# First chunk of a linear attention and gated FFN kernel: VectorE's work ordered behind an earlier gate product, a task's loads ahead of weight loads

## The chip, the cores and the metric

The kernel runs on one core of a Trainium2 chip. The core has TensorE (matmuls), VectorE, ScalarE, GpSimd, and SyncE, which issues the DMAs. The metric is the device time in microseconds of one execution; the median of three runs is given.

## The reference

A linear attention is followed by a gated feed-forward layer. The softmax of q runs over the 64 elements of a head, that of k over the 576 positions.

```python
# q, k, v: (8, 8, 576, 64) float32
q_s = softmax(q, axis=-1); k_s = softmax(k, axis=2)
kv = einsum('bhsd,bhse->bhde', k_s, v)
x = einsum('bhsd,bhde->bhse', q_s, kv)      # then rows of 512: (4608, 512)
out = (x @ w_a) * (x @ w_b) @ w_out          # d_ff = 1536
```

The weights arrive as float64 and are turned into float32 on the chip.

## The kernel before

The 4608 rows are worked on in nine chunks of 512. Later chunks use a fast matrix product with seven products per pair of 128-wide tiles of d_ff; the first chunk, which the change touches, does it plainly, tile by tile, while it converts the weights.

The first chunk has twelve tiles f of 128 columns of d_ff. For tile f, "gate f" is 24 matmuls (L510) into two PSUM banks, `k0` for x @ w_a and `k1` for x @ w_b. ScalarE copies the first bank into `ga` (`gate_half`, L517), VectorE multiplies it by the second (`gate_end`, L521, the "product of gate f"), and `project_first` (L545) multiplies the result by w_out. Gate f+1 writes the same two banks, so its first half needs ScalarE's copy of gate f and its second half needs the product of gate f.

A float64 weight block becomes float32 in `float_parts`: two ScalarE casts (L103, L104), a VectorE shift (L107), a GpSimd addition (L110), a VectorE join (L113). For w_a and w_b a split into an upper part (ScalarE, L79, or L920 in the startup) and a lower part (VectorE, L82, or L925) follows, which gate f reads; blocks of w_out are split by `split_wo` only for the later chunks. Buffers are few: four `wr`, eight `wy`, eight `ws`, eleven `xo`, which raw weights share.

Beside this, "tasks" prepare the attention for the next chunk: keys (0, 1, 3 and 5), queries (2, 4, 6 and 7), and one key task of a later batch (8). A task has a load, a softmax part (`soft`: for keys a maximum L292 and an exponential; for queries a maximum L358, eight short exponentials L361, L365, L366 and a GpSimd product L367), a transpose on TensorE (`turn`) and a product.

Up to gate 2 the steps stand in an order written out by hand, and `in_order` keeps that order on ScalarE, VectorE and GpSimd (and for the first loads on SP). `in_order` also fixes TensorE's order through the whole first chunk. Everything else is placed by a scheduler at build time, which simulates the engines and may put an instruction of a later loop pass into any gap of an engine's queue; each engine then works its queue strictly in that order. `tc.issue_after(ins)` holds instructions that are traced in its block, and run on the engine of `ins`, behind `ins` in that order; instructions of other engines are free.

The loop over f from 2 to 11 traces, in each pass, the loads of tile f+2, the conversion of w_out's block f, the conversion of w_a and w_b for tile f+1, a load of task f-1, the turn of task f-3, the softmax part of task f-2, gate f (from f = 3), the product of task f-3, and the projection of tile f-1. The lines around the change are these:

```python
    tasks[0][0]()
    load_f(3)
    tasks[1][0]()
```

They stand in the prologue, so task 1 is loaded there, and in the loop's first pass (n + 2 = 1) once more. Before, the softmax parts were held only behind the last splits of the startup, `startup[0]` on ScalarE and `startup[1]` on VectorE. In the last pass the first two blocks of w_out are split and the operands of chunk 1 are made (`x_operands`, with L484 to L494), while GpSimd adds up weights for the fast product (`sums`, L225).

Of the kernel before, what the change touches and what calls it, by code (L numbers as in the profile page):

```python
# [13 lines left out]
ALU = mybir.AluOpType  # L14
# [15 lines left out]
def linear_attention_then_gated_ffn(  # L30
# [18 lines left out]
    nc = tc.nc  # L49
# [4 lines left out]
    NF = 2 * NI  # L54
# [21 lines left out]
    def split(hi, lo, src, hi_engine="act"):  # L76

        if hi_engine == "act":
            nc.scalar.copy(out=hi, in_=src)  # L79
        else:  # L80
            nc.vector.tensor_copy(out=hi, in_=src)
        return nc.vector.tensor_tensor(out=lo, in0=src, in1=hi.bitcast(F32), op=ALU.subtract)  # L82
# [4 lines left out]
    def float_parts(raw, y=None):  # L87

        top = raw.bitcast(F32).rearrange("p (n t) -> p n t", t=2)[:, :, 1]
        low = raw.bitcast(U32).rearrange("p (n t) -> p n t", t=2)[:, :, 0]
        if y is None:
            y = sb.tile([P, DM], F32, name="wy", bufs=8)
        r = sb.tile([P, DM], I32, name="wr", bufs=4)
        u = raw.bitcast(I32)[:, 0:DM]
        yi = y.bitcast(I32)  # L100

        def both():
            nc.scalar.activation(out=y, in_=top, func=AF.Copy, scale=2.0 ** -112)  # L103
            nc.scalar.activation(out=r, in_=low, func=AF.Copy, scale=2.0 ** -29)  # L104

        def shift():
            nc.vector.tensor_single_scalar(u, yi, 3, op=ALU.logical_shift_left)  # L107

        def add():
            nc.gpsimd.tensor_tensor(out=r, in0=u, in1=r, op=ALU.add)  # L110

        def join():
            nc.vector.scalar_tensor_tensor(  # L113
                out=yi, in0=yi, scalar=-(2 ** 31), in1=r, op0=ALU.bitwise_and, op1=ALU.bitwise_or
            )

        return y, (both, shift, add, join)

    def to_float(raw):
        y, parts = float_parts(raw)  # L120
        for part in parts:
            part()
        return y
# [3 lines left out]
    def load_f(f):  # L127

        i, r = divmod(f, 2)
        for half in range(2):  # L130
            raw = sb.tile([P, DM], I64, name="raw", tag="xo", bufs=11)
            ins = nc.sync.dma_start(out=raw, in_=w_ab[i, r, half])
            raws[f, half] = raw
        raw = const.tile([P, DM], I64, name=f"wo{f}_raw", tag=f"wo{f}")
        with tc.issue_after(ins.ins):
            nc.sync.dma_start(out=raw, in_=w_out[f])
        raws[f, "o"] = raw
        return ins
# [3 lines left out]
    def wo_home(f):  # L142
        if f > 3:
            return None
        if f > 1:
            if "mr" not in raws:
                raws["mr"] = sb.tile([P, 2, DM], F32, name="yo", tag="mr", bufs=2)
            return raws["mr"][:, f - 2]
        return sb.tile([P, DM], F32, name=f"yo{f}", tag=f"u{f + 2}", bufs=1)

    def keep_wo(f, y):
        if f > 3:
            w = const.tile([P, 2, DM], F32R, name=f"wo{f}_w", tag=f"wo{f}")
            nc.sync.dma_start(out=w[:, 1].bitcast(F32), in_=y)
            wo[f] = w
            y = w[:, 1].bitcast(F32)
        wo_first[f] = y

    def convert_wo(f):
        y, parts = float_parts(raws.pop((f, "o")), wo_home(f))  # L160
        for part in parts:
            part()
        keep_wo(f, y)

    def split_wo(f):
        if f < 4:
            wo[f] = const.tile([P, 2, DM], F32R, name=f"wo{f}_w", tag=f"wo{f}")
        split(wo[f][:, 0], wo[f][:, 1], wo_first[f])
# [14 lines left out]
    def convert_ab(f, half):  # L183

        keep_ab(f, half, *whole_ab(f, half, to_float(raws.pop((f, half)))))

    def whole_ab(f, half, y):
        w = ws_tile()
        yv = y.rearrange("p (n c f) -> p n c f", n=2, c=2)
        split(w[:, :, 0], w[:, :, 1], yv)  # L190
        return y, w

    def keep_ab(f, half, y, w):
        i, r = divmod(f, 2)
        dy[i, r, half] = dr.tile([P, DM], F32, name=f"dy{i}{r}{half}")
        nc.sync.dma_start(out=dy[i, r, half], in_=y)
        op = ((A11, A12), (None, A22))[r][half]
        if op is not None:
            put_w(i, op, w)
        blocks[f, half] = w  # L200
# [301 lines left out]
    def gate_banks(tags):  # L502
        return [ps.tile([P, T], F32, name=f"pt{n}", tag=tag) for n, tag in enumerate(tags)]

    def gate_part(f, x, n, pairs, pt):

        for g in pairs:
            w = blocks[f, g // 2][:, n, :, g % 2]
            for i, (wp, xp) in enumerate(((0, 0), (0, 1), (1, 0))):
                nc.tensor.matmul(  # L510
                    pt, w[:, wp], x[g][:, xp],
                    start=(g == 0 and i == 0), stop=(g == NP - 1 and i == 2),
                )
# [4 lines left out]
        return ga  # L518

    def gate_end(ga, pt):  # L520
        nc.vector.tensor_tensor(out=ga, in0=pt, in1=ga, op=ALU.mult)  # L521

    def g_split(f, g):
        gh = sb.tile([P, T], F32R, name=f"gh{f % 2}", bufs=1)
# [207 lines left out]
    def key_task(g):  # L732
        box = {}

        def load():
            box["k"] = k_load_t(1, g)
            box["v"] = v_load(1, g)

        def soft():
            kv_exp_t(box["k"])  # L740

        def turn():
            box["e"], copy = kv_turn(box["k"], ("k2", "at"))
            return [copy]

        def prod():
            kv_whole(1, g, box["e"], box["v"], "at")

        return load, soft, turn, prod

    def query_task(g):
        box = {}

        def load():
            box["q"] = q_load(1, g)

        def soft():
            q_soft_first(box["q"])

        def turn():  # L760
            box["e"], copy = q_whole(box["q"], "k2", g % 2)
            return [copy]

        def prod():
            px = x_whole(1, g, box["e"], "at")
            nc.scalar.copy(out=xfs[1][:, g], in_=px)

        return load, soft, turn, prod

    def late_key_task(g, tag="k2"):  # L770
        box = {}

        def load():
            box["k"] = k_load(2, g)
            box["v"] = v_load(2, g)

        def soft():
            box["m"] = kv_max(box["k"])

        def turn():  # L780
            box["m"] = kv_max_turn(box["m"], tag)

        def back():
            kv_exp(box["k"], kv_max_all(box["m"], tag))

        def prod():
            kv_split(2, g, kv_product(box["k"], box["v"], "at"))

        return load, soft, turn, back, prod

    tasks = [key_task(0), key_task(1), query_task(0), key_task(2), query_task(1), key_task(3),
             query_task(2), query_task(3)] + [late_key_task(g) for g in range(1)]
# [13 lines left out]
    at = {}  # L806

    class Startup:
# [153 lines left out]
            at["ga", f] = gate_half(f, at["pt", f][0])  # L962

        def G(f):
            gate_end(at["ga", f], at["pt", f][1])

    x0 = [None] * NP
    traced = nc.cur_bb.bb.instructions
# [35 lines left out]
    startup = [at["last", 0].ins, at["last", 1].ins]  # L1004

    po = at["po"]
    pending = (1, at["ga", 1])
    for f in range(2, NF):
        if f + 2 < NF:
            load_f(f + 2)  # L1010
        convert_wo(f)
        if f + 1 < NF:
            convert_ab(f + 1, 0)
            convert_ab(f + 1, 1)


        n = f - 3
        if n + 2 < NF - 3:
            tasks[n + 2][0]()
        if n < 0:  # L1020
            copies = ()
        else:
            copies = tasks[n][2]()
        if n + 1 < NF - 3:
            with tc.issue_after(startup[0]), tc.issue_after(startup[1]):
                tasks[n + 1][1]()
        if f == NF - 1:
            split_wo(0)
            split_wo(1)
            sy[0] = sums(0)  # L1030
            x_operands(xfs[1], early + late, xo)
        if f > 2:
            pts = gate_banks(("k0", "k1"))
            for h in range(2):
                gate_part(f, x0, h, range(NP), pts[h])
                if h == 0:
                    with ExitStack() as pinned:
                        for copy in copies or ():
                            pinned.enter_context(tc.issue_after(copy.ins))
                        at["ga", f] = gate_half(f, pts[0])  # L1040
            gate_end(at["ga", f], pts[1])
        if n >= 0:
            tasks[n][3]()
        project_first(*pending, po)
        pending = (f, at["ga", f])
# [16 lines left out]
    for c in range(1, NCH):  # L1062
# [4 lines left out]
        for i in range(NI):  # L1067
# [32 lines left out]
            end = c == NCH - 1 and i == NI - 1  # L1100
# [78 lines left out]
```

## Time and profile before

| | |
|---|---|
| time, median of 3 runs | 979.13 us (978.07 to 979.45) |
| the profiled execution | 979.73 us, span 977.9 us |
| TensorE busy (matmul) | 946.1 us, 97% of the span |
| TensorE busy (weight load) | 846.8 us, 87% |
| VectorE busy | 626.7 us, 64% |
| ScalarE busy | 392.0 us, 40% |
| GpSimd busy | 112.3 us, 11% |
| TensorE's mean granted clock | 0.993 of full |

The span is the profile's stretch from the first to the last instruction; the time holds what lies around it too. Shares are means over the whole span, of which the first chunk is some 17%. In the trace PE is TensorE, DVE VectorE, ACT ScalarE, POOL GpSimd, and SP or SPq SyncE and its queue; L521 is line 521 of the kernel. A row of a timeline shows where an instruction starts, how long it lasts, what it writes and reads, and in brackets how long its engine was idle before it and what ended the wait.

### The profile page before, as it was taken

The numbers are of one execution on the slowest core, as the hardware profiler recorded it, in microseconds if no ns is written. First come the engines' busy times: TensorE is split into PE (matmuls) and PEld (weight loads), VectorE is DVE, ScalarE is ACT, GpSimd is POOL, SyncE is SP. The second block draws the span as 40 slices with busy tenths as digits, with TensorE's granted clock in tenths as the row PEclk, the third lists the DMA queues.
The fourth block names the chain that finished last, engine by engine and source line by source line (L and its number), as shares of the span: only waits on it lengthen the run. The fifth ranks groups of instructions, "written<-read, shape, count | busy, mean of one in ns | idle before, by whom it ended". The sixth has DMA issues, their size and how long they took to land.

```text
span 977.9 us, 16984 instructions
## 1 busy us (share of the span) xinstructions
PE 946.1 (97%) x6159; PEld 846.8 (87%) x6159; DVE 626.7 (64%) x1241; ACT 392.0 (40%) x1085; POOL 112.3 (11%) x96
## 2 busy tenths in 40 slices
PE   5879999899999999999999999999999999999998
PEld 4656666799999999999999999999999999999997
DVE  6985777986686656666576566565666446653433
ACT  7875764552363324432442235223623263221101
POOL 3453344332000000000000000000000000000000
PEclk9989999999999999999999999999999999999999
DMA  9999675989898977997699779877988688767761
GB/s 344 412 380 341 238 242 198 408 306 352 290 334 280 361 253 248 334 359 264 240 343 340 257 256 339 299 304 257 331 276 293 236 314 274 271 219 279 255 206 56
DMA packets 97874, 283.26 MB, mean 290 GB/s; under 512 B 11712, under 2 KB 12288, under 8 KB 97792
## 3 DMA queue, kind: packets, MB, share of 16 engines
q1 hardware_dynamic: 97792, 282.18, 80.4%
q8 instruction: 49, 0.80, 0.3%
q14 instruction: 33, 0.27, 0.1%
HBM read 242.06 MB, written 37.98 MB: 286 GB/s over the span
## 4 chain that ended last, share of the span: by engine, by line
PE 80%; DMA 8%; DVE 5%; issue 3%; POOL 2%; ACT 2%; SPq 1%; POOLq 0%; DVEq 0%
PE po L556 27%; PE ka L535 13%; PE kp L535 13%; PE kx L535 13%; PE ky L535 7%; PE pk L312 3%; PE px L466 2%; DMA dw<-ws 2%; POOL wr L110 2%; DMA qts<-in_q 1%; PE pt L510 1%; DMA wo_raw<-in_w_out 1%; DMA vt<-in_v 1%; DMA mr<-dq 1%; PE po L545 1%
## 5 line engine op out<-in xcount | busy, mean ns | idle before, releaser
L556 PE MATMUL po<-wo_w,gh 128*128 128x512 f32 x768 | 230.1, 396 | 0.0
L535 PE MATMUL kx<-xo,ws 128*128 128x256 f32 x1152 | 162.8, 283 | 1.0 <-DVE cc L1110 0.8
L535 PE MATMUL ka<-xo,ws 128*128 128x256 f32 x1152 | 161.4, 283 | 0.8 <-DVE u L1095 0.8
L556 PEld LDWEIGHTS po<-wo_w,gh 128*128 128x128 f32 x768 | 138.6, 188 | 26.8 <-ACT gh L79 0.6
L535 PE MATMUL kp<-xo,ws 128*128 128x256 f32 x1152 | 157.2, 283 | 1.4 <-DVE u L1095 1.4
L535 PEld LDWEIGHTS ka<-xo,ws 128*128 128x128 f32 x1152 | 149.7, 188 | 4.9 <-DVE u L1095 1.0
L535 PEld LDWEIGHTS kx<-xo,ws 128*128 128x128 f32 x1152 | 149.3, 188 | 4.0 <-DVE cc L1110 1.0
L535 PEld LDWEIGHTS kp<-xo,ws 128*128 128x128 f32 x1152 | 146.9, 188 | 3.8 <-issue 1.6
L556 PE MATMUL po<-wo_w,gl 128*128 128x512 f32 x384 | 139.2, 395 | 0.0
L79 ACT CAST gh<-cc 128x512 fp32r<-128x512 f32 x96 | 57.5, 620 | 131.5 <-DVE cc L1119 118.0
L1118 DVE TENSOR_TENSOR cc<-kp,u 128x512 f32<-128x512 f32 x48 | 33.2, 691 | 102.3 <-PE kp L535 102.3
L1109 ACT COPY cc<-kx 128x256 f32<-128x256 f32 x48 | 17.8, 371 | 180.9 <-PE kx L535 174.3
L380 ACT ACTIVATE qt<-qt,st 128x64 f32<-128x64 f32 x224 | 74.9, 338 | 27.6 <-DVE st L377 21.5
L556 PEld LDWEIGHTS po<-wo_w,gl 128*128 128x128 f32 x384 | 71.5, 188 | 16.5 <-DVE gl L82 0.4
L510 PE MATMUL pt<-xo,ws 128*128 128x512 f32 x288 | 75.4, 418 | 9.8 <-DVE ga L521 5.0
L510 PEld LDWEIGHTS pt<-xo,ws 128*128 128x128 f32 x288 | 56.0, 198 | 25.2 <-DVE ga L521 5.4
L535 PE MATMUL ky<-xo,ws 128*128 128x256 f32 x576 | 77.4, 283 | 0.3 <-DMA ws<-dw 0.3
L1108 DVE TENSOR_TENSOR cc<-kp,u 128x512 f32<-128x512 f32 x48 | 32.9, 686 | 68.1 <-PE kp L535 67.9
L535 PEld LDWEIGHTS ky<-xo,ws 128*128 128x128 f32 x576 | 71.8, 188 | 1.1 <-issue 0.5
L82 DVE TENSOR_TENSOR gl<-cc,gh 128x512 fp32r<-128x512 f32 x96 | 66.9, 704 | 8.3 <-ACT gh L79 8.1
L244 POOL PARTITION_ALL_REDUCE mx<-m x20 | 14.7, 736 | 460.2 <-DVE m L255 421.7
L1094 ACT COPY u<-kx 128x512 f32<-128x512 f32 x48 | 28.0, 583 | 82.0 <-PE kx L535 82.0
(144 smaller groups left out, 1202.7 us busy)
## 6 DMA issues: line engine op xcount, KB each, us to landing
ws<-dw SPq DMA_DIRECT2D x312, 512.0 KB, 5.4
dw<-ws SPq DMA_DIRECT2D x42, 512.0 KB, 6.2
mr<-dq SPq DMA_DIRECT2D x112, 128.0 KB, 3.9
raw<-in_w_ab SPq DMA_DIRECT2D x24, 512.0 KB, 7.5
vt<-in_v SPq DMA_DIRECT2D x29, 325.0 KB, 7.4
out<-ot SPq DMA_DIRECT2D x36, 256.0 KB, 5.0
qt<-in_q SPq DMA_DIRECT2D x32, 256.0 KB, 5.4
kt<-in_k SPq DMA_DIRECT2D x24, 320.0 KB, 5.3
```

Source lines behind the costliest of these rows:

```text
L79: nc.scalar.copy(out=hi, in_=src)
L82: return nc.vector.tensor_tensor(out=lo, in0=src, in1=hi.bitcast(F32), op=ALU.subtract)
L110: nc.gpsimd.tensor_tensor(out=r, in0=u, in1=r, op=ALU.add)
L312: nc.tensor.matmul(pk, kt[:, j].rearrange("p h d -> p (h d)"), vt[:, j], start=(j == 0), stop=(j == J - 1),)
L380: nc.scalar.activation(out=qt[:, j, h], in_=qt[:, j, h], func=AF.Exp, bias=st[:, h, 0, j:j + 1], accum_out=st[:, h, 1, j:j + 1],)
L466: nc.tensor.matmul(px[:, s], w, m[:, s], start=(i == 0), stop=(i == 2))
L510: nc.tensor.matmul(pt, w[:, wp], x[g][:, xp], start=(g == 0 and i == 0), stop=(g == NP - 1 and i == 2),)
L535: ins = nc.tensor.matmul(pt[:, n], w[:, n, wp, c], x[:, xp, c], start=(first and n == 0 and i == 0), stop=(i == 5), skip_group_check=True,)
L556: ins = nc.tensor.matmul(po[t], a[:, ts], wo[f][:, w], start=(f == 0 and i == 0), stop=(f == NF - 1 and i == 2),)
L1094: nc.scalar.copy(out=u2, in_=kx)
L1108: nc.vector.tensor_tensor(out=cc[:, 3], in0=kp, in1=u3, op=ALU.add)
L1118: nc.vector.tensor_tensor(out=cc[:, 1], in0=kp, in1=u2, op=ALU.add)
```

## The change

- The product of each gate is kept in `at["end", f]`, those of the startup and those of the loop.
- In pass f the conversions of w_out's block f and of tile f+1 are traced inside `issue_after(at["end", f - 2].ins)`. That instruction runs on VectorE, so their VectorE steps (shift, join, lower part) stand behind the product of gate f-2.
- The softmax part of task f-2 stands, with its VectorE steps, behind the product of gate f-2 (in pass 2, behind that of gate 1) instead of behind the last split of the startup. Its ScalarE steps stay behind `startup[0]`.
- The splits of w_out's blocks 0 and 1 stand, with their VectorE half, behind the product of gate 10.
- A task's load is traced ahead of `load_f(f + 2)`, under the condition `1 < f - 1 < NF - 3`, so tasks 2 to 8 are loaded in passes 3 to 9, and task 1 only in the prologue.

```diff
@@ -518,7 +518,7 @@
         return ga
 
     def gate_end(ga, pt):
-        nc.vector.tensor_tensor(out=ga, in0=pt, in1=ga, op=ALU.mult)
+        return nc.vector.tensor_tensor(out=ga, in0=pt, in1=ga, op=ALU.mult)
 
     def g_split(f, g):
         gh = sb.tile([P, T], F32R, name=f"gh{f % 2}", bufs=1)
@@ -962,7 +962,7 @@
             at["ga", f] = gate_half(f, at["pt", f][0])
 
         def G(f):
-            gate_end(at["ga", f], at["pt", f][1])
+            at["end", f] = gate_end(at["ga", f], at["pt", f][1])
 
     x0 = [None] * NP
     traced = nc.cur_bb.bb.instructions
@@ -1006,27 +1006,30 @@
     po = at["po"]
     pending = (1, at["ga", 1])
     for f in range(2, NF):
+        if 1 < f - 1 < NF - 3:
+            tasks[f - 1][0]()
         if f + 2 < NF:
             load_f(f + 2)
-        convert_wo(f)
-        if f + 1 < NF:
-            convert_ab(f + 1, 0)
-            convert_ab(f + 1, 1)
+
+        with tc.issue_after(at["end", f - 2].ins):
+            convert_wo(f)
+            if f + 1 < NF:
+                convert_ab(f + 1, 0)
+                convert_ab(f + 1, 1)
 
 
         n = f - 3
-        if n + 2 < NF - 3:
-            tasks[n + 2][0]()
         if n < 0:
             copies = ()
         else:
             copies = tasks[n][2]()
         if n + 1 < NF - 3:
-            with tc.issue_after(startup[0]), tc.issue_after(startup[1]):
+            with tc.issue_after(startup[0]), tc.issue_after(at["end", max(f - 2, 1)].ins):
                 tasks[n + 1][1]()
         if f == NF - 1:
-            split_wo(0)
-            split_wo(1)
+            with tc.issue_after(at["end", f - 1].ins):
+                split_wo(0)
+                split_wo(1)
             sy[0] = sums(0)
             x_operands(xfs[1], early + late, xo)
         if f > 2:
@@ -1038,7 +1041,7 @@
                         for copy in copies or ():
                             pinned.enter_context(tc.issue_after(copy.ins))
                         at["ga", f] = gate_half(f, pts[0])
-            gate_end(at["ga", f], pts[1])
+            at["end", f] = gate_end(at["ga", f], pts[1])
         if n >= 0:
             tasks[n][3]()
         project_first(*pending, po)
```

## Rows read from the trace of the kernel before

**Rows 1.** Page, part 2: the span in 40 equal slices, tenths.
```profile
PE   5879999899999999999999999999999999999998
...
PEclk9989999999999999999999999999999999999999
```

**Rows 2.** TensorE's order of time: start us, us, engine line op, tiles, shapes, count, [idle before].
```profile
43.61 0.74 PE L510 MATMUL pt<-xo,ws 128*128 128x512 f32 x2 [1.74 <-ACT ws L920]
46.18 6.92 PE L510 MATMUL pt<-xo,ws 128*128 128x512 f32 x22 [1.83 <-DVE ws L925]
...
60.27 3.04 PE L510 MATMUL pt<-xo,ws 128*128 128x512 f32 x12
68.30 5.49 PE L510 MATMUL pt<-xo,ws 128*128 128x512 f32 x12 [4.99 <-DVE ga L521]
...
132.42 5.83 PE L510 MATMUL pt<-xo,ws 128*128 128x512 f32 x24
...
143.55 5.82 PE L510 MATMUL pt<-xo,ws 128*128 128x512 f32 x24
...
163.04 0.49 PE L271 MATMUL pmx<-m,ones 128*128 128x128 f32 x2 [1.68 <-DVE m L265]
```

**Rows 3.** Busy time by windows: engines, granted clock, DMA share, GB/s.
```profile
47.00:48.00 1.00, 1.00 (x4) 0.81 (x3) 1.00 (x3) 1.00 (x4) 0.00 (x0) 0.50 1.01 406
...
68.00:70.00 2.00, 1.71 (x4) 1.43 (x5) 1.77 (x4) 1.13 (x3) 0.74 (x1) 0.50 0.96 325
```

**Rows 4.** VectorE's order of time up to gate 2's product.
```profile
34.92 0.68 DVE L82 TENSOR_TENSOR wo_w<-yo,wo_w 128x512 fp32r<-128x512 f32 x1
...
37.66 1.86 DVE L107 TENSOR_SCALAR wo_raw<-yo 128x512 int32<-128x512 int32 x2
...
44.97 1.15 DVE L925 TENSOR_TENSOR ws<-wy,ws 128x512 fp32r<-128x512 f32 x1
...
46.77 1.26 DVE L358 TENSOR_REDUCE qst<-qt 128x8 f32<-128x512 f32 x2
...
50.92 2.39 DVE L82 TENSOR_TENSOR wo_w<-yo,wo_w 128x512 fp32r<-128x512 f32 x2
...
62.50 1.51 DVE L107 TENSOR_SCALAR raw<-wy 128x512 int32<-128x512 int32 x1
...
64.14 1.24 DVE L365 TENSOR_SCALAR qst<-qst 128x8 f32<-128x8 f32 x1
...
67.56 0.68 DVE L521 TENSOR_TENSOR ga<-pt,ga 128x512 f32<-128x512 f32 x1
```

**Rows 5.** ScalarE's order of time ahead of gate 2's copy.
```profile
47.62 0.33 ACT L361 ACTIVATE qt<-qt,qst 128x64 f32<-128x64 f32 x1
...
58.73 0.34 ACT L361 ACTIVATE qt<-qt,qst 128x64 f32<-128x64 f32 x1
...
59.56 0.58 ACT L517 COPY ga<-pt 128x512 f32<-128x512 f32 x1
```

**Rows 6.** SP's queue, order of time.
```profile
38.25 0.33 SPq L285 DMA_DIRECT2D kt<-in_kt  x1
```

**Rows 7.** Waits of SP's queue, 0 to 200 us: total, times, longest.
```profile
SPq L285 <- PE pk L312: 2.9, 1, 2.9
```

**Rows 8.** VectorE's order of time, later tiles and the change of chunks.
```profile
106.61 0.69 DVE L521 TENSOR_TENSOR ga<-pt,ga 128x512 f32<-128x512 f32 x1 [0.92 <-PE pt L510]
...
119.60 1.17 DVE L82 TENSOR_TENSOR ws<-wy,ws 128x512 fp32r<-128x512 f32 x1 [0.66 <-ACT ws L79]
...
141.73 0.65 DVE L521 TENSOR_TENSOR ga<-pt,ga 128x512 f32<-128x512 f32 x1
...
149.48 0.69 DVE L521 TENSOR_TENSOR ga<-pt,ga 128x512 f32<-128x512 f32 x1 [5.24 <-PE pt L510]
...
151.61 1.76 DVE L489 TENSOR_TENSOR xt<-xf 128x512 f32<-128x512 f32 x1
```

**Rows 9.** GpSimd's order of time at the change of chunks.
```profile
146.99 12.64 POOL L225 TENSOR_TENSOR ws_y<-ws_y 128x512 f32<-128x512 f32 x8 [3.91 <-DMA ws_y<-dy]
```

## The prediction

> **What bounds the kernel now.** I read the slices of the page first. Each slice is 24.4 us. TensorE is busy nine tenths or more from the fourth slice on, but for the eighth, and the third slice (48.9 to 73.3 us) stands out: seven tenths busy, and the only one whose granted clock is under nine tenths [rows 1]. The first eight slices hold the first chunk and the change to the second; behind them TensorE runs through. A change in the first chunk is therefore worth what it does to TensorE's idle time and clock there, and the 780 us behind it only move. I then read TensorE's own order of time in the first chunk [rows 2]. Its order is fixed by the code, so each idle stretch names what was late. Three stretches matter. Gate 2 (tile f=2) waits 1.74 us for ScalarE's upper part of a weight (L920) and 1.83 us for VectorE's lower part (L925). The second half of gate 3 waits 4.99 us, from 63.31 to 68.30, for VectorE's product of gate 2 (L521), which frees its PSUM bank. At the change of chunks the product pmx waits 1.68 us for VectorE (L265). Behind the first two the granted clock is 0.50 [rows 3], the lower of the two levels, 1.2 GHz.
>
> Last I read VectorE's order ahead of that late product [rows 4]. Gate 2's matmuls are over by 53.1 us (46.18 + 6.92), yet the product starts at 67.56. VectorE is not waiting for it: it works through an in-order queue in which pieces of much later tiles stand in front.
>
> **The change part by part.**
>
> *A. The product of gate 2.* Loop pass f now puts its VectorE conversions and its task's exponents behind the product of tile f-2 (at least tile 1 for the exponents). Before gate 2's product only passes 2 and 3 may now stand. What leaves its front, with the durations of [rows 4]: the statistics of two query tasks, which belong to passes 4 and 6 (1.26 us for two maxima, then two additions of 1.24 us each, of which the last is shown), the split of w_out block 0 (half of the 2.39 us of two splits, 1.20), and the first shift of tile 5's weights (1.51). Together 1.26 + 2 x 1.24 + 1.20 + 1.51 = 6.45 us; durations overlap by some 0.07 us in a row, so I count 6.1. The product moves from 67.56 to at most 61.5 and ends by 62.2, in front of the 63.31 at which TensorE wants the bank. It also needs ScalarE's copy of the first half, which starts at 59.56 [rows 5]. That copy stood behind 16 short exponentials of the same two query tasks, 0.33 us each, 5.3 us in all; they need the statistics just moved, so they leave too, and the copy can come near 54 us. TensorE's wait of 4.99 us goes. Hiding margin: 63.31 - 62.2 = 1.1 us; if that cover is gone, every us of lateness is one of TensorE.
>
> *B. The clock behind that wait.* Twelve matmuls took 5.49 us behind the wait and 3.04 us in front of it [rows 2]; the clock was 0.50 in the first case [rows 3]. Without the wait: 5.49 - 3.04 = 2.45 us back. The Trainium skill, "TensorE: Matmul & The Clock Gate", section "What's actually happening", says that how many matmuls run cold behind an idle stretch varies from run to run; no run here repeats this stretch. By that rule the term could be left out, and the sum would end 2.45 us higher. I take the row. A + B = 7.44 us.
>
> *C. Gate 2 itself.* Before its last weight part (VectorE at 44.97) stood one w_out split (0.68, block 1, at 34.92) and one of the two w_out shifts at 37.66 (half of 1.86, 0.93), both of the loop and both now behind gate 0's product [rows 4]. The shift also starts a GpSimd addition in the same stretch. So the part comes 1.6 us earlier at least by these two. Bounds: below nothing gained (the scheduler may put other unpinned work there), above both waits and the slow clock, 1.74 + 1.83 + 6.92 - 22/24 x 5.83 = 5.15 us (5.83 is 24 matmuls at full clock [rows 2]). I take 2.5, half of it, above the 1.6 since the clock would follow.
>
> *D. Splits of w_out 0 and 1.* They leave stretches where VectorE was ahead of need and come behind gate 10's product (149.48), just where VectorE makes the operands of the next chunk [rows 8]. A two-input VectorE operation takes 0.68 us there or, while GpSimd's eight additions run (146.99 to 159.63 [rows 9]), 1.76 us [rows 8]. Bounds: 0, if they are put behind the operands; 2 x 1.76 = 3.5, if all of it reaches the wait of pmx (163.04 [rows 2]), which ends on VectorE. I take 2 x 0.68 = 1.4: two operations more in a row push the last two of the row out of GpSimd's stretch, where they are fast. The Trainium skill, "GPSIMD Engine Reference", section "1. Specifications", says that GpSimd shares its SBUF interfaces with VectorE instructions that have two SBUF inputs; by that alone both splits would cost the slow price, 3.5, and the sum would end 2.1 us higher. The rows show both prices on the two sides of the additions' end.
>
> *E. Loads.* A task's load (one DMA for a query, two for a key) now stands in front of pass f's three weight loads on SP's queue instead of behind them. A key load that waits for its buffer holds SP: 2.9 us once [rows 7], and behind it stand weight loads and the write-backs that free conversion buffers. Raw weights are loaded some tiles ahead of their conversion, so I take 0; what would be late next is a conversion, with 12 us of lead (below). One thing falls away: task 1 was loaded in the prologue and again in pass 2 (kt at 38.25 [rows 6], then vt), 320 and 325 KB by their shapes. At 406 GB/s [rows 3] that is 1.6 us of full queues. TensorE waits for VectorE and ScalarE there, not for loads, so I take 0; bounds 0 and 1.6 gained.
>
> *F. The conversions held back.* From tile 6 on they already stood behind the product of the tile two before. Tile 9: product 6 at 106.61, its last weight part at 119.60 to 120.77, gate 9 at 132.42 [rows 2, 8]. So a chain takes 13.5 us behind the product (120.77 - 107.30) and is 11.7 us ahead of need: holding it costs nothing. The other danger is VectorE falling behind once TensorE comes earlier. Product 9 starts at 141.73, 3.5 us behind the end of its matmuls (132.42 + 5.83); TensorE wants its bank in gate 10's second half, 143.55 + 2.9 = 146.45 [rows 2, 8], 4.0 us behind the product's end. If TensorE moved 8 us and VectorE not at all, 4 us would be given back. I take 0, since the products that now gate VectorE's work move with TensorE; bounds 0 and 4.
>
> **Sum.** The profiled execution took 979.73 us, with a span of 977.9; 979.73 - 7.44 - 2.5 + 1.4 = 971.2. The median of the runs is 0.6 us below the profiled one, so 970.6.
>
> **The rivals.**
>
> *Given back in the second half.* A and B come, but VectorE is the next to be late between 120 and 165 us: F costs 2 to 4, D 1.4 to 3.5. For it speaks product 9's lag; against it the 5.24 us that VectorE stands idle for TensorE ahead of product 10 [rows 8]. Middle values: -7.44 + 3 + 2.5 from 979.1 is 977.2 without C, 974.7 with it; I write 976.
>
> *The product stays late.* The change doesn't say where unpinned work goes: the splits of w_out 2 and 3, which the next chunk asks for, and a task's copy of transposed keys may still stand in front of it. If 2.7 us of the wait stays, the clock still falls, the gain is 2.3 and D takes 1.4: 978.2, within what can be told from no change (0.2%, 2 us). Against it: 6.1 us leave VectorE's queue, and 67.56 + 0.68 - 63.31 = 4.9 suffice.
>
> *Slower.* ScalarE's instructions are not pinned. If the new order puts ScalarE's copy of gate 2 behind casts of tile 4's weights, which wait for VectorE's joins now held behind products 0 and 1, the product waits for the copy instead. It decides where the copy ends later than 67.56, 7.4 us behind its present end of 60.14 [rows 5]. With a copy 10 us later than now, product 2 is 2.6 us later, D adds 1.4, C nothing: 983. For it speaks that the copy is already 6.4 us behind its matmuls; against it the 5.3 us of exponentials that leave ScalarE's queue.
>
> **How the numbers follow.** Forecast 0.65 (970.6, own range 965.5 to 974.5); given back 0.13 (976); product stays late 0.10 (978.2); slower 0.12 (983). The lower end: -7.44 - 5.15 - 1.6 with D at 0.7 is 965.5. The upper end reaches past the second case and the nearer half of the third, 978.3; beyond lie the slower case and some 0.05 of the third, and 0.03 below. Faster by over 0.2% (under 977.2): forecast and given back, 0.78. Within: 0.10. Slower: 0.12.
>
> **What would show it.** Right: no wait of TensorE for L521 in the gate of f=3, its twelve matmuls in about 3.0 us, granted clock 1.00 there; VectorE's query maxima (L358) behind the product of gate 2; gate 4 starting 7 to 13 us earlier than before; about 1.4 us more ahead of pmx. Wrong: a new wait of TensorE in front of gate 3 to 5 for weight parts (L79, L82) or for ScalarE's copy, products 8 and 9 far behind their matmuls, or the whole lead gone by 190 us.

## The result, and the profile after

The changed kernel is slower by 0.4%: a median of 983.04 us (980.54 to 990.14, 20 runs) against 979.29 (977.49 to 985.73, 20 runs) of the kernel before beside it; ratio 1.0041, 95% interval 1.0025 to 1.0057. The prediction said 970.6, with a range of 965.5 to 978.3. The profiled execution took 982.48 us, with a span of 980.7.

The page's part 2 for the changed kernel (40 slices of 24.5 us) says that the third slice's dip [rows 1] is gone, as was forecast, and that the granted clock is nine tenths or more everywhere. A new dip stands in the fourth slice (73.5 to 98 us), seven tenths busy.

```profile
PE   5997998899999999999999999999999999999998
...
PEclk9999999999999999999999999999999999999999
```

TensorE's order of time in the changed kernel, beside [rows 2]:

```profile
41.85 0.74 PE L510 MATMUL pt<-xo,ws 128*128 128x512 f32 x2 [0.58 <-ACT ws L920]
43.67 5.38 PE L510 MATMUL pt<-xo,ws 128*128 128x512 f32 x22 [1.09 <-DVE ws L925]
...
56.23 5.83 PE L510 MATMUL pt<-xo,ws 128*128 128x512 f32 x24
63.03 1.36 PE L312 MATMUL pk<-vt,kt 128*128 128x130 f32 x10 [0.98 <-ACT qt L361]
...
69.30 0.30 PE L299 MATMUL pkb<-ident,kt 128*128 128x128 f32 x1 [1.04 <-DVE wholes L323]
69.36 5.83 PE L510 MATMUL pt<-xo,ws 128*128 128x512 f32 x24
...
79.93 5.82 PE L510 MATMUL pt<-xo,ws 128*128 128x512 f32 x24
...
95.48 1.12 PE L299 MATMUL pka<-ident,kt 128*128 128x128 f32 x4 [5.32 <-ACT kt L293]
...
96.46 7.73 PE L510 MATMUL pt<-xo,ws 128*128 128x512 f32 x24
...
108.93 5.84 PE L510 MATMUL pt<-xo,ws 128*128 128x512 f32 x24
...
151.35 5.83 PE L510 MATMUL pt<-xo,ws 128*128 128x512 f32 x24
159.99 1.69 PE L535 MATMUL kx<-xo,ws 128*128 128x256 f32 x12 [2.82 <-ACT ga L517]
161.78 0.49 PE L271 MATMUL pmx<-m,ones 128*128 128x128 f32 x2
```

Gate 2 waits 0.58 and 1.09 us where it waited 1.74 and 1.83, and its 22 matmuls take 5.38 instead of 6.92. Gate 3 runs its 24 matmuls in one piece, without the wait of 4.99 and the half clock. So what terms A, B and C count on has come. Two new waits, 0.98 us for a query's exponentials and 1.04 us for VectorE, stand between gate 3 and gate 4. In the kernel before the same gates start as follows:

```profile
78.72 5.83 PE L510 MATMUL pt<-xo,ws 128*128 128x512 f32 x24
89.30 5.82 PE L510 MATMUL pt<-xo,ws 128*128 128x512 f32 x24
...
100.24 0.66 PE L299 MATMUL pka<-ident,kt 128*128 128x128 f32 x4 [0.70 <-ACT kt L293]
...
111.31 5.82 PE L510 MATMUL pt<-xo,ws 128*128 128x512 f32 x24
...
153.64 5.83 PE L510 MATMUL pt<-xo,ws 128*128 128x512 f32 x24
```

The lead is 78.72 - 69.36 = 9.36 us at gate 4, 9.37 at gate 5, 2.38 at gate 7 and 2.29 at gate 11. Seven microseconds go at one place: the transpose `pka` ahead of gate 6 waits 5.32 us for an exponential instead of 0.70 and takes 1.12 us instead of 0.66, and gate 6 behind it takes 7.73 us instead of 5.81 (granted clock 0.62 from 96 to 102 us).

The rest of the loss lies where the prediction looked at nothing. The last output copies (L569) of chunks 0 and 2, changed kernel:

```profile
172.02 0.58 ACT L569 COPY ot<-po 128x512 f32<-128x512 f32 x1 [0.27 <-PE po L545]
...
391.14 0.58 ACT L569 COPY ot<-po 128x512 f32<-128x512 f32 x1
```

and of the kernel before:

```profile
173.29 0.58 ACT L569 COPY ot<-po 128x512 f32<-128x512 f32 x1 [0.27 <-PE po L545]
...
387.95 0.58 ACT L569 COPY ot<-po 128x512 f32<-128x512 f32 x1
```

A lead of 1.27 us at the end of chunk 0 is a lag of 3.19 at the end of chunk 2: the stretch between the two copies took 219.12 us instead of 214.66. Behind it both need nearly the same to the end of the span, 589.6 us in the changed kernel and 590.0 before. So the lead was spent at gate 6, to a smaller part (1.0 us) at the change from chunk 0 to chunk 1, and in chunks 1 and 2, mostly at the change from the one to the other. That last place is read best in the chain of waits, here of the changed kernel, from the second query's product `px` on (start us, us, what):

```profile
258.43 0.76 PE px L466 x5
...
259.22 0.70 DVE xf L658
...
261.08 6.21 DMA mr<-dq
...
267.41 0.70 DVE qtt L427
...
269.32 4.92 PE po L556 x20
274.24 0.06 PE px L466
...
277.51 0.63 ACT xo L79
...
278.18 0.58 PE ky L535
```

Read downwards: the product of query 2 is multiplied by VectorE into `xf`, which frees one of two `mr` buffers; only then can the DMA of the statistics of the fourth query start (6.21 us); then come its exponential, its product, and from this the operands of chunk 2. The fourth query's product stands among the last 24 matmuls of the projection (`po`), so when its result turns into operands TensorE has nothing left to do, and `ky` waits 2.16 us. In the kernel before the end of the chain is almost only TensorE:

```profile
272.06 5.81 PE po L556 x24
277.87 0.12 PE ky L535
```

There the product stands ahead of the 24 matmuls, and they cover the operands. The last part of the product's operand, `ql`, comes from VectorE, and TensorE waits for it; kernel before:

```profile
270.29 0.69 DVE L82 TENSOR_TENSOR ql<-qtt,qh 128x512 fp32r<-128x512 f32 x1
271.03 0.33 PE L466 MATMUL px<-ql,kvh 128*128 128x128 f32 x1 [0.86 <-DVE ql L82]
```

and in the changed kernel:

```profile
270.51 0.69 DVE L82 TENSOR_TENSOR ql<-qtt,qh 128x512 fp32r<-128x512 f32 x1
```

The operand is complete at 271.20 us instead of 270.98, so it is hardly later than before. What differs is TensorE's order: before, the product is issued as soon as its operand is there; in the changed kernel it stands behind 20 matmuls that start at 269.32, and begins at 274.24.

### The profile page after: what moved, and what is told of

Read it like the earlier page. It is cut to its first block, busy times and chain, and to the rows that moved or that the text cites. A ratio compares the mean times of both kernels' runs of the same rounds, so it can differ in the third digit from the quotient of the medians.

```text
span 980.7 us, 16987 instructions
## 1 busy us (share of the span) xinstructions
PE 944.9 (96%) x6159; PEld 845.4 (86%) x6159; DVE 634.7 (65%) x1241; ACT 392.5 (40%) x1085; POOL 113.0 (12%) x96
## 4 chain that ended last, share of the span: by engine, by line
PE 79%; DVE 7%; DMA 7%; ACT 3%; issue 2%; SPq 1%; POOL 0%; DVEq 0%; ACTq 0%; POOLq 0%
PE po L556 26%; PE ka L535 13%; PE kp L535 13%; PE kx L535 13%; PE ky L535 7%; PE pk L312 3%; PE px L466 2%; DMA dw<-ws 1%; PE pt L510 1%; DMA kt_first<-in_kt 1%; DMA mr<-dq 1%; DVE wy L113 1%; DVE raw L107 1%; PE po L545 1%; SPq L421 1%
## 5 line engine op out<-in xcount | busy, mean ns | idle before, releaser
L510 PE MATMUL pt<-xo,ws 128*128 128x512 f32 x288 | 73.3, 410 | 2.4 <-DVE ws L925 1.1
L82 DVE TENSOR_TENSOR gl<-cc,gh 128x512 fp32r<-128x512 f32 x96 | 65.4, 689 | 8.2 <-ACT gh L79 8.1
```

The lines of the kernel that those rows point to most:

```text
L510: nc.tensor.matmul(pt, w[:, wp], x[g][:, xp], start=(g == 0 and i == 0), stop=(g == NP - 1 and i == 2),)
```

## The experiments

Sixteen kernels ran, in four groups; each ratio is to runs of the kernel before on the same chip. "Stretch" is the time between the last output copies of chunks 0 and 2 in the profiled execution; "product late" says whether the fourth query's product stands among the last matmuls of chunk 1's projection.

| kernel | second load of task 1 | product late | stretch, us | median, us | ratio (95% interval) |
|---|---|---|---|---|---|
| before | kept | no | 214.66 | 979.0 to 979.4 | 1 |
| changed | dropped | yes | 219.12 | 983.04 | 1.0041 (1.0025 to 1.0057) |
| e1, drop alone | dropped | yes | 218.62 | 983.45 | 1.0043 (1.0026 to 1.0059) |
| e2, three pins | kept | no | 212.16 | 977.41 | 0.9980 (0.9964 to 0.9997) |
| e3, three pins and the key maximum first | kept | yes | 217.74 | 987.35 | 1.0073 (1.0048 to 1.0099) |
| e4, e3 without the split pin | kept | yes | 214.82 | 986.52 | 1.0072 (1.0057 to 1.0086) |
| e5, changed without the split pin | dropped | no | 212.14 | 976.59 | 0.9975 (0.9956 to 0.9994) |
| e6, conversions and softmax pinned | kept | yes | 220.68 | 981.58 | 1.0020 (1.0002 to 1.0038) |
| e7, conversions pinned alone | kept | no | 213.93 | 975.03 | 0.9948 (0.9930 to 0.9966) |
| e8, order of the loads alone | kept | no | 214.63 | 978.34 | 0.9990 (0.9971 to 1.0009) |
| e13, changed, rows in another buffer | dropped | no | 212.44 | 979.35 | 0.9983 (0.9963 to 1.0003) |
| e14, before, rows in another buffer | kept | no | 211.52 | 976.61 | 0.9965 (0.9948 to 0.9982) |
| e15, drop alone, rows in another buffer | dropped | no | 213.10 | 975.07 | 0.9945 (0.9927 to 0.9963) |
| e16, e7, rows in another buffer | kept | no | 213.14 | 974.20 | 0.9931 (0.9905 to 0.9957) |

e9 to e12 follow below; their stretches are 223 to 225 us.

**First group: the dropped load, and the key maximum ahead.** The drop alone, in the kernel before:

```diff
-        if n + 2 < NF - 3:
+        if 1 < n + 2 < NF - 3:
             tasks[n + 2][0]()
```

> Only the second load of task 1 is dropped; nothing is pinned. Theory A (dropping it makes the scheduler place the later chunks anew, and that new order loses time between 190 and 340 us): about 4 us slower than before (the changed kernel lost 1.26 + 2.75 = 4.0 us from ky at 165 us to the end), with waits of TensorE for ScalarE or the weight DMAs around 270 to 330 us as in the changed kernel. Theory B (that loss comes from the first chunk's pins): within 1 us of before, no such waits.

983.45 us, as theory A said: with no pin at all this one condition gives a loss as large as that of the changed kernel. What the prediction set down as work saved (0 to 1.6 us gained) goes with 4.3 us lost, though the first chunk is ahead here too (the last copy of chunk 0 at 171.90, and gate 3 waits 1.66 us instead of 4.99). The stretch is 218.62.

The opposite, all three pins with the loads as before, e2:

> All three pins of VectorE's work, but loads placed as before, with task 1 loaded twice. Theory A: the later chunks run as in the kernel before, the 1.3 us of lead at 165 us stays, 978 us, 5 us under the changed kernel; the wait of TensorE for key task 3's exponential (5.3 us in the changed kernel) stays. Theory B: 982 to 983 as the changed kernel.

977.41 us, ratio 0.998. The same wait at gate 6 is there (6.45 us for L293), yet the kernel is faster than before, since its stretch is 212.16. Theory A's time is met, but not by its route: the later chunks don't run as in the kernel before (214.66), and the lead at the last copy of chunk 0 is 0.43 us, not 1.3 (the profiled execution lost some 4 us again later, of which 2.68 us are one wait for a weight's DMA at 426 us).

For the wait at gate 6, e3 puts the conversions of a pass behind the maximum (L292) of the key task of the pass before, and the product of a gate behind the maximum of its own pass, with the load kept (an excerpt; the maximum's instruction is also handed back by its function):

```diff
-        with tc.issue_after(at["end", f - 2].ins):
+        behind = at.get(("soft", f - 1)) or at["end", f - 2]
+        with tc.issue_after(at["end", f - 2].ins), tc.issue_after(behind.ins):
             convert_wo(f)
...
-                tasks[n + 1][1]()
+                at["soft", f] = tasks[n + 1][1]()
...
-            at["end", f] = gate_end(at["ga", f], pts[1])
+            with ExitStack() as ahead:
+                if ("soft", f) in at and at["soft", f] is not None:
+                    ahead.enter_context(tc.issue_after(at["soft", f].ins))
+                at["end", f] = gate_end(at["ga", f], pts[1])
```

> As e2, and VectorE's maximum of each task is held ahead of the product of its pass's gate, the next conversions behind it. Theory C (TensorE's 5.3 us wait in front of gate 6 is VectorE's order: the maximum stands behind conversions although its keys are there): the wait and the half clock behind it (1.9 us) go, 971 us, 7 us under e2. Theory D (the keys land late, or the conversions behind are the next to be late): VectorE waits for the key load in that place, or TensorE waits for weight parts; 976 us or more.

e4 is e3 without the pin of the splits:

> As e3, without the pin on the splits of w_out blocks 0 and 1, which the scheduler may place early again. Theory E (the two splits behind product 10 delay ScalarE's copy of gate 11 and so the first product of chunk 1, 2.8 us in the changed kernel): that wait under 0.5 us, 1.5 to 3 us under e3. Theory F (GpSimd's additions and the operands set that place whatever stands there): within 0.5 us of e3.

987.35 and 986.52 us. The wait at gate 6 falls to 2.43 us in both, but the work that was pushed back is late elsewhere. TensorE's order in e3:

```profile
93.81 0.67 PE L300 MATMUL pka<-ident,kt 128*128 128x128 f32 x4 [2.43 <-ACT kt L293]
...
120.89 0.33 PE L300 MATMUL pkb<-ident,kt 128*128 128x128 f32 x1 [3.76 <-ACT xf L767]
...
163.91 0.80 PE L271 MATMUL pmx<-m,ones 128*128 128x128 f32 x2 [4.46 <-DVE m L265]
```

VectorE in e3, ahead of the first of these waits:

```profile
91.47 0.69 DVE L82 TENSOR_TENSOR wo_w<-wo_w 128x512 fp32r<-128x512 f32 x1 [9.99 <-PE po L546]
92.08 0.81 DVE L292 TENSOR_REDUCE mc<-kt 128x1 f32<-128x640 f32 x1
```

So the forecast of a gain failed. In these plans a split of w_out, which nothing pins, stands right ahead of the maximum, and VectorE is idle for 9.99 us until TensorE's projection lets it run; whether the maximum without that split would keep the lead of gate 5 is not shown. For the split pin the two give neither E's nor F's forecast (0.8 us apart); a cleaner pair for it follows.

**Second group: is it the load, or the plan?** The late query product stands in the changed kernel, in e1, e3 and e4, and not in e2 or the kernel before. Two variants cross the two: one drops the load and has the product early, the other keeps the load and has it late.

e5 is the changed kernel without the pin of the splits, e6 is e2 without it:

```diff
-            with tc.issue_after(at["end", f - 1].ins):
-                split_wo(0)
-                split_wo(1)
+            split_wo(0)
+            split_wo(1)
```

> The changed kernel without the pin on the splits of w_out 0 and 1; the second load of task 1 stays dropped. In its order the last query product of the change from chunk 1 to 2 (L466) is issued well ahead of the last block of the projection, as in the kernel before, and not among it, as in the changed kernel. Theory P (the change costs its time where that product is issued late; dropping the load only happened to give that order): no wait of 2.2 us for ScalarE's L79 near 278 us, time 976.5 to 979.5. Theory L (the dropped load itself makes the plan of the later chunks worse, as the run with the drop alone at 983.45 suggests): 982 to 985. Both expect a wait of some 5 to 6 us at gate 6 for the exponential of key task 3.

> Conversions and softmax parts pinned as in the changed kernel, splits of w_out and all loads as before. Here the last query product of the change from chunk 1 to 2 is issued late, among the projection's last block, although the second load is kept. Theory P: waits for L79 of about 2.2 us near 278 us as in the changed kernel, time 980 to 983. Theory L: the load is kept, so like the run with the load kept (977.4): 976 to 979.

976.59 with the load dropped and 981.58 with it kept: both as theory P said, and both against theory L (the wait at gate 6 is 3.96 us in e5, not 5 to 6). TensorE in e6, as in the changed kernel:

```profile
269.56 2.12 PE L556 MATMUL po<-wo_w,gh 128*128 128x512 f32 x8 [2.27 <-ACT gh L79]
...
278.43 0.39 PE L535 MATMUL ky<-xo,ws 128*128 128x256 f32 x1 [2.16 <-ACT xo L79]
```

So the dropped load as such doesn't cost the time. It changes the order that the scheduler finds for the next chunks, and so do the pins.

e2 and e6 also price the split pin, by which alone they differ: gate 11 starts at 151.50 and 151.72 us, the last copy of chunk 0 at 172.86 with the pin and at 170.61 without. In the changed kernel and e5 it is 20.67 and 18.64 us from the one to the other. So the pin costs 2.0 to 2.5 us at the change of chunks in these plans; in e3 and e4, where `pmx` waits over 4 us with the pin and without, it is 0.6.

e7 pins the conversions alone:

> Only the conversions are pinned behind the product of two tiles ago; softmax parts, splits and loads as before. Query maxima stand ahead of gate 2's product again. If the conversions' pin alone frees that product, TensorE's wait in gate 3 is under 1 us and gate 4 starts at 69 to 71; if the query tasks were the larger part of what stood in front of it, the wait stays at 3 to 5 us and only gate 2 itself is faster (2 to 3 us). Key task 3's maximum stands three instructions behind product 5, so the wait at gate 6 is under 2 us. Time 975 to 978 in either case by theory P and L alike (early query product, load kept); 979 or more would say that a lead of the first chunk is worth nothing at the end.

975.03 us, the fastest so far. TensorE's order in e7:

```profile
57.89 3.06 PE L510 MATMUL pt<-xo,ws 128*128 128x512 f32 x12 [1.17 <-ACT ga L517]
61.54 3.05 PE L510 MATMUL pt<-xo,ws 128*128 128x512 f32 x12 [0.59 <-DVE ga L521]
...
72.24 0.30 PE L299 MATMUL pkb<-ident,kt 128*128 128x128 f32 x1 [2.66 <-DVE wholes L323]
72.30 5.84 PE L510 MATMUL pt<-xo,ws 128*128 128x512 f32 x24
...
95.06 0.66 PE L299 MATMUL pka<-ident,kt 128*128 128x128 f32 x4 [1.95 <-ACT kt L293]
```

Gate 3 waits 1.76 us in two parts, neither under 1 nor 3 to 5 as expected, and gate 4 starts at 72.30; the wait at gate 6 is under 2 us. So the conversions' pin gives 3.2 of the 4.99 us of term A, all of B (12 matmuls in 3.05 us) and all of C, with the two query maxima still ahead of product 2 (44.53 us, the product at 60.81).

e8 has the order of the loads alone:

```diff
     for f in range(2, NF):
+        if f - 1 < NF - 3:
+            tasks[f - 1][0]()
         if f + 2 < NF:
...
-        if n + 2 < NF - 3:
-            tasks[n + 2][0]()
```

> Only the order of the loads changes: a task's loads ahead of the weights' loads, the second load of task 1 kept. TensorE, VectorE and ScalarE have the order of the kernel before. If the order of the loads is free, as the prediction took it: ratio 1.000 within 0.002, 978 to 980. If key loads that wait for a buffer hold the weights' loads behind them: 980 to 983, with waits of conversions for raw weights.

978.34 us, ratio 0.999 (0.9971 to 1.0009): no difference, as term E took it.

**Third group: the product pinned ahead.** From the fourth query's product on, chunk 1's projections stand behind it (an excerpt; `at["last x"]` is that product's last matmul):

```diff
-            project(f, ghl, po, c == NCH - 1 and f >= NF - 2)
+            with ExitStack() as pinned:
+                if c == 1 and "last x" in at:
+                    pinned.enter_context(tc.issue_after(at["last x"].ins))
+                project(f, ghl, po, c == NCH - 1 and f >= NF - 2)
```

> The changed kernel with one more pin: from the last query product of chunk 2 (L466) on, the projections of chunk 1 stand behind that product. The first chunk keeps its order on every engine; the product now stands ahead of all 24 matmuls of the last block, not among them. Theory P: the waits of 0.56 and 2.16 us near 270 and 278 us and the half clock behind them (some 2 us) go, a wait of TensorE for the product's operand of up to 1.5 us comes, and the time is 977.5 to 980.5. Rival R (the late product is only a sign of a plan whose later chunks cost more in other places): 982 to 984.

> The same pin in the kernel with conversions and softmax parts pinned, splits and loads as before (981.58 without it). Theory P: 977 to 980. Rival R: 981 to 983.

> The same pin in the kernel that only drops the second load of task 1 (983.45 without it). Its first chunk is 1.4 us ahead of the kernel before at the last output row of chunk 0. Theory P: 978 to 981. Rival R, and the theory that the dropped load itself costs time: 982 to 985.

> Control: the same pin in the kernel before, whose last query product already stands ahead of the last block. Theory P: within 1.5 us of the kernel before (978 to 980.5). If the pin itself is a gain whatever the order (by re-planning of the later chunks), it is 975 to 977, and the gains of the three others are not the late product's.

990.84, 985.32, 987.97, and 988.39 for the control: all slower, the control by 9 us (ratio 1.0089, 1.0074 to 1.0105). No forecast of P or R holds. TensorE in e12:

```profile
271.31 0.47 PE L466 MATMUL px<-qh,kvh 128*128 128x128 f32 x1 [6.71 <-ACT qh L79]
```

The product now stands early and waits for its operand: 6.71 us here, 5.25, 5.07 and 4.91 in the others. But the pin did more than set the product ahead. In the kernel before 24 of chunk 1's projection matmuls stand behind the product; in e12 48 do. The 24 that moved had filled TensorE's time ahead of it: TensorE comes to the product at 264.60 us (269.95 before), while the operand's upper part is ready at 271.3 (269.4 before). So the group doesn't decide between P and R. It doesn't acquit the late place either: in the changed kernel the operand was there 3 us before the product was issued. What it shows is the bound on an earlier place, the chain that brings the operand.

**Fourth group: the chain's first link taken away.** The rows of statistics of the fourth query get two of the eight `wy` buffers, so that their DMA needs no `mr` buffer to come free (early chunks alone; the others had such buffers before):

```diff
-        if roomy(c):
+        if roomy(c) or g >= 3:
             rows = [sb.tile([P, T], F32, name=f"mr{w}", tag="wy", bufs=8) for w in range(2)]
```

> The changed kernel, with the rows of statistics of the fourth query of each early chunk in two of the eight wy buffers, so that their DMA (mr from dq) doesn't wait until VectorE has multiplied the second query's product (xf, L658). The first chunk keeps its order on every engine. Theory C (a chain sets the change from chunk 1 to 2: second query's product, its multiplication, the DMA of 7.5 us into the buffer this frees, exponential and split, fourth query's product, operands of the next chunk): the waits of 0.56 and 2.16 us near 270 and 278 us go, the stretch from the last output copy of chunk 0 to that of chunk 2 falls from 219.1 to 213 to 215 us, time 977 to 979.5. Rival R (the plan of the later chunks costs in other places): 981 to 984.

> Control: the same buffers in the kernel before. Theory C: there the chain reaches TensorE only as 0.86 us near 271 us, so 977.5 to 979.5, and the changed kernel with these buffers is no longer slower than this one. Rival R: the distance between the two stays at 3 to 4 us.

> The same buffers where only the second load of task 1 is dropped (983.45 without them). Theory C: 977 to 979.5, its first chunk being 1.4 us ahead of the kernel before. If the dropped load costs time of its own: 981 to 984.

> The same buffers where only the conversions are pinned (975.03 without them, its wait near 267 us being 0.71): theory C 973.5 to 975.5, as the chain costs it little; rival R gives no forecast.

TensorE at the same place in e13:

```profile
267.99 0.22 PE L466 MATMUL px<-qh,kvh 128*128 128x128 f32 x1
...
274.12 0.28 PE L535 MATMUL ky<-xo,ws 128*128 128x256 f32 x1
...
275.27 1.47 PE L535 MATMUL ky<-xo,ws 128*128 128x256 f32 x11
```

Neither the product nor `ky` waits, and `ky` starts 4.06 us earlier than in the changed kernel (274.12 against 278.18). The stretch falls from 219.12 to 212.44 us, and in the kernel that only drops the load from 218.62 to 213.10, its time from 983.45 to 975.07 (expected: 977 to 979.5). So the dropped load costs nothing here: e15 is no slower than e14. For the waits near 270 and 278 us theory C holds. It is not separated from theory P, since the product also stands ahead of the projection's last block again. And the buffers do more than shorten the chain: in the kernel before, where the chain's wait was 0.86 us, the stretch falls by 3.1 us and the time to 976.61, under the 977.5 expected, and the waits near 330 us, which are not of the chain, are gone in e13 and e14. In e7 the stretch falls by 0.8.

One part of the expectations failed. The changed kernel with these buffers was to be no slower than the control; its median is 2.7 us above it, close to the 3 to 4 us of rival R (by the ratios 1.8 us, with overlapping intervals, 0.9963 to 1.0003 and 0.9948 to 0.9982). The two profiled executions have the same span of 973.8 us and reach the end of chunk 2 within 0.1 us (384.14 and 384.07), but the profiled one of e13 is its fastest: four of its twelve executions took 975.6 to 976.4 us, eight 979.3 to 980.8 (mean granted clocks 0.992 to 0.995 and 0.990 to 0.993), and no trace shows those eight. So for the changed kernel rival R is not excluded; for the kernel that only drops the load it is.

e16 is the fastest kernel of the study: 974.20 us, ratio 0.9931.

## Why the prediction was wrong

**Terms A, B and C** held in mechanism; that their sum fits is partly luck. VectorE in the changed kernel ends the queue ahead of gate 2's product earlier than [rows 4]:

```profile
58.22 0.68 DVE L521 TENSOR_TENSOR ga<-pt,ga 128x512 f32<-128x512 f32 x1
```

The product starts at 58.22 instead of 67.56 (the prediction: at most 61.5), and ScalarE's copy at 55.37 (forecast near 54). The forecast lead was 4.99 + 2.45 + 2.5 = 9.94 us, the measured one 9.36 at gate 4. But C gave more than its 2.5: gate 2's matmuls end at 49.05 instead of 53.10, a lead of 4.05. Then A and B came in full, and the two new waits ahead of gate 4, which no term has, took 0.98 + 1.04 = 2.02. The two misses nearly cancel. What A names as the cause was only partly right: e7 gives 3.2 of the 4.99 us while the query maxima still stand in front.

**The first step that failed is F**, "holding it costs nothing". Its 11.7 us of lead were read from one weight part of one tile, and the step named product 9 as the next thing late. The softmax parts, held behind the same products, are counted in A alone, as a gain; that the maxima of later key tasks now wait there, behind the conversions traced ahead of them, has no term. What was late next was the exponential of key task 3 ahead of gate 6. VectorE there, changed kernel:

```profile
87.76 0.68 DVE L521 TENSOR_TENSOR ga<-pt,ga 128x512 f32<-128x512 f32 x1
88.50 1.05 DVE L107 TENSOR_SCALAR wo_raw<-wy 128x512 int32<-128x512 int32 x1
...
93.76 0.81 DVE L292 TENSOR_REDUCE mc<-kt 128x1 f32<-128x640 f32 x1
```

and in the kernel before:

```profile
95.16 0.69 DVE L521 TENSOR_TENSOR ga<-pt,ga 128x512 f32<-128x512 f32 x1
...
98.51 0.81 DVE L292 TENSOR_REDUCE mc<-kt 128x1 f32<-128x640 f32 x1
```

The maximum of key task 3 stood 3.35 us behind product 5 and stands 6.00 behind it now, with five instructions of conversions between instead of three. In e7, where the softmax parts are free, three stand between and it is 3.17 us. The maximum came 98.51 - 93.76 = 4.75 us earlier, TensorE at gate 5 9.37 us, and this accounts for the wait: 0.70 + 9.37 - 4.75 = 5.32 us, as measured; 1.92 us of slow clock came on top. (This is a balance of both traces and no forecast: the 4.75 are known only afterwards.) The row at 100.24 with its wait of 0.70 us for L293 was in the trace of before; the prediction passed over it. A wait of 0.7 us is a place without slack: of any lead that TensorE brings there, all is lost that the releaser doesn't gain too. The rival "given back in the second half" is the nearest: it set such a loss 25 us too late, and F's part of it at 2 to 4 us, where 7.0 went.

**Term D** was too small and misplaced: 2.0 to 2.5 us by e2 and e6 and by the changed kernel and e5, where the prediction took 1.4 between bounds of 0 and 3.5. The two splits at the change of chunks took 3.13 us together (147.79, L82), beside GpSimd's additions (144.69 to 150.38). The Trainium skill, "GPSIMD Engine Reference", section "1. Specifications", whose rule of shared SBUF interfaces the prediction set aside at 2.1 us, came nearer to these 3.13 us than the 1.4. The cost did not show at `pmx`, which no longer waits, but one step ahead: `kx` waits 2.82 us for ScalarE's copy of gate 11, which starts at 159.36, behind the cast of an operand that VectorE makes after the splits and three casts of added weights. Of the lead of 2.29 us at gate 11, 1.27 are left at the last copy of chunk 0.

**The second step that failed is E with the sentence "the 780 us behind it only move".** By its own work the dropped load costs nothing, as E took it (e15 is 1.5 us faster than e14, with overlapping intervals), and so does the loads' order (e8). But chunks 1 and 2 did not only move: the scheduler ordered them anew, and the new order put the chain query 2's product, `mr` DMA, fourth query's product, operands on the path, with the product behind 20 matmuls of the projection. The stretch grew by 4.46 us: 2.16 + 0.56 - 0.86 of waits near 270 us, some 1.65 of slow matmuls behind (the first `ky` and `ka`, at 278.18 and 278.78, 0.58 each and eleven `ky` at 279.16 2.52, where e13's rows have 0.28 and 1.47; the granted clock is 0.91 from 270 to 290 us), and 0.94 of a longer wait near 330 us, which is not of this chain: TensorE waits 1.76 us there for a weight's DMA, where it waited 0.82 for VectorE.

The sum, on the profiled executions: 9.36 won at gate 4; 7.0 lost at gate 6; 1.1 at the change of chunks; 4.46 in chunks 1 and 2; 0.4 won behind. That is a loss of 2.8 us, as 982.48 against 979.73 shows. The rival on the slower side named another mechanism (gate 2's copy behind casts), which did not come; the time of 983 fits it by chance. (The lower end of the range comes to 965.6 by its own terms, not 965.5.)

What stays open is, first, why the scheduler's plan places the fourth query's product late in some variants. No run sets the product ahead in the changed kernel and leaves all else as it is, so what its place alone costs there isn't measured. Nor is it known what eight of e13's executions spend 3 to 5 us on. The late place alone doesn't set the stretch either: e4 has it, with its 2.16 us of wait, and a stretch of 214.82, where the other late ones have 217.7 to 220.7 and the early ones without a new buffer 212.1 to 214.7.

## What to carry to other kernels

Before a lead is counted, walk down the fast engine's order and note every wait, however short: each marks a step without slack, and a lead is lost there unless the releaser moves too (0.70 + 9.37 - 4.75 = 5.32). So forecast the releaser's lead as well, and count what else is held behind the same instruction ahead of it. Where a scheduler orders the rest, an edit of one stage re-orders the others, so compare the stretches between fixed marks, such as the last output copy of each chunk, before explaining a difference by the edit. Before an instruction that stands late is forced ahead, look when its operand is complete, and at all that the pin holds back: in the kernel before the pin also moved 24 matmuls behind the product and cost 9 us, while a buffer for the first link of the chain lowered the median by 2.8 to 8.4 us in three of four kernels and by 0.8 in the fourth.

## What the runs showed of the hardware

VectorE's operations cost more beside GpSimd's additions also inside the first chunk: a shift with one input took 1.05 us at 88.50 and 1.49 at 90.07, while GpSimd made three additions between 87.98 and 93.28, and 0.43 us at 87.42, ahead of the additions. The `mr` DMA of 128 KB took 6.21 us in the chain, with the DMA engines' busy share at 1.01 from 261 to 267.3 us. Waits of TensorE of like length were followed by slow matmuls in some places and not in others: behind 2.16 us the first `ky` took 0.58 us (0.28 in e13), with a granted clock of 0.53 from 278 to 280 us, while behind the 2.66 us at 72.24 in e7 the 24 matmuls of gate 4 took 5.84 us at a granted clock of 1.00.
